# Dealing out the P @ V blocks: at most three (or four) behind each third slot instead of all that is due

## The chip, the cores and the metric

The kernel runs on one core of a Trainium2 chip. The metric is the device time of one execution in microseconds (us), median of several runs; lower is better. The engines are named as in the profile: PE (TensorE, matmuls; PEld its weight loads), DVE (VectorE), ACT (ScalarE), POOL (GpSimd), SP (SyncE, which issues nearly all DMAs).

## The reference

The input is one sequence `x` of 2048 tokens of 512 values. Two attention branches of 32 heads of 16 dimensions each are mixed by a gate per token:

```python
g = sigmoid((x * gate_w).sum(-1, keepdims=True))
a = A(x)      # full softmax attention: softmax(q k^T / 4) v over all 2048 keys, then @ A_wo
b = B(x)      # per segment of 512 tokens: causal softmax attention inside the segment,
              # blended with a memory (phi(q) M / phi(q) z) of the segments before, then @ B_wo
return g * a + (1 - g) * b
```

So for 512 queries a head of A has 2048 keys to score, a head of B 512, of which the causal mask leaves about half. All numbers are float32.

## The kernel before

**Stages.** First the projections: `x` times the weights, as high and low float32r halves, in 64 matmul slots (`slot`, L311). They end about 342 us into the profiled execution. Then comes the attention phase, which is what the change touches.

**Units and slots.** A unit is a branch, a group of four heads and a chunk `c` of 512 queries: 32 units of A and 32 of B, mostly in turn. An A unit has 64 slots (4 heads times 16 blocks of 128 keys), a B unit 10, so a pair has 74 and the phase has 2368 slots. The loop at the end of `gated_mix` runs over the slots `n`. In each it does two things:

- `score_part(n)` (L619 the matmul, L642 and L639 the exponential): scores of one key block against 512 queries into a PSUM tile `st` (three buffers), and ACT's `exp` of it into one quarter of a tile `p` (four buffers, each for four slots).
- `max_part(n + 96)` (L204 the matmul; L219, L234, L240, L244 the reduction): for a unit further on, scores into a PSUM tile `sm` (four buffers), whose row maxima DVE takes. The maximum is put into the operands of the scores later, so that `exp` needs no second pass. The last 96 slots have no such part.

The two matmuls of a slot sit on different halves of PE's rows (partitions 0 to 49 and 64 to 113) and can run side by side.

**P @ V.** When four slots of a unit have been scored, four blocks of work are put into `queue`: block `i` stands for 128 queries of all four heads against one key block, and it is due three slots later (five for B). `some_values` (L654) takes what is due and makes runs: neighbouring blocks of the same four become one run of four matmuls, one per head, each on its own 32 columns of PE (`tile_position`), with 17 weight columns (16 dimensions and a column of ones for the sum) and 128 to 512 query columns. They are float32, so each matmul is two in the trace: a run is eight matmuls, whatever its width. All runs add into one PSUM tile `ops`; after the last block of a unit ACT copies it (L679, `oraw`) and it is stored.

**What sets the order.** Every engine works its instructions in the order in which this loop emits them. `some_values` is called behind each third slot (`BURST = 3`). There it competes with `fill`: a list of output products with their due slots (L758 `fin`, eight matmuls of 512 columns each, 36 times; and L890 in the last chunk). When a fill is due, it takes that place (`filled`), P @ V is left out there, and the blocks wait. Fills come 33 slots apart in chunks 0 and 1 and 24 apart in chunk 2. `run_late` (L194, `mt_ps`) transposes finished maxima through an `st` buffer, 64 times.

Of the kernel before, what the change touches and what calls it, by code (L numbers as in the profile page):

```python
# [34 lines left out]
NU = 32  # L35
LEAD = 96
BURST = 3
RUN = 8
GAP = {"A": 3, "B": 5}
MASK_T = 8  # L40
# [6 lines left out]
def gated_mix(ctx, tc, x, xT, wqkv, a_wo, b_wq, b_wk, b_wv, b_wo, beta, gate_w, out):  # L47
# [59 lines left out]
    nS = len(slots)  # L107
# [143 lines left out]
    def run_todo(m):  # L251

        for e in [e for e in todo if e[0] <= m]:
            todo.remove(e)
            e[1]()

    def run_late(pool, tag, m):
        for e in [e for e in late if e[0] < m]:
            late.remove(e)
            transpose_max(e[1], e[2], pool, tag)  # L260
# [3 lines left out]
    def loads(m):  # L264

        m = min(m, len(maxs) - 1)
        while loaded[0] <= m:
            u, (r, i) = maxs[loaded[0]]
            if loaded[0] == first_max[u]:
                load_q(u)  # L270
            kc = u[2] if u[0] == "B" else i // 8
            if (u, kc) not in kt_:
                load_k(u, kc)
            loaded[0] += 1
# [329 lines left out]
    queue = []  # L604

    def score_part(n):

        u, j = slots[n]
        side, g, c = u
        q = qt[u]  # L610

        if j % 4 == 0:
            pt_[u, j // 4] = pp.tile([128, 4, CH], F32, tag="p", name="p")
        p = pt_[u, j // 4]
        h = (0, 2, 1, 3)[j % 4]

        def score(ps, h, b, k, n0, q0):

            nc.tensor.matmul(ps[:, n0:n0 + CH - q0], rows(k[:, :, b * 128:(b + 1) * 128], h, 50),  # L619
                             rows(q[:, :, q0:], h, 50), start=True, stop=True)  # L620

        def diagonal(x):
            nc.gpsimd.affine_select(out=x, in_=x, pattern=[[0, 4], [1, 128]], base=0, channel_multiplier=-1,  # L623
                                    compare_op=ALU.is_ge, fill=0.0)

        ps = st_ps.tile([128, CH], F32, tag="st", name="st")
        if side == "A":
            score(ps, h, j // 4 % 4, kt_[u, j // 16], 0, 0)
        else:
            k = kt_[u, c]  # L630
            if j < 8:
                score(ps, h, j // 4, k, 0, 128 * (j // 4))
                if j >= 4:
                    score(ps, h, 3, k, 384, 384)
            else:
                for f in range(2):
                    score(ps, 2 * (j - 8) + f, 2, k, 256 * f, 256)
        if side == "B" and j >= 8:
            nc.scalar.activation(p[:, 2 * (j - 8):2 * (j - 8) + 2, 0:256], ps.rearrange("p (h t) -> p h t", h=2), AF.Exp,  # L639
                                 scale=SCALE)  # L640
        else:
            nc.scalar.activation(p[:, h], ps, AF.Exp, scale=SCALE)  # L642
        if j % 4 == 3 or j == SLOTS[side] - 1:
            if side == "B":
                diagonal(p[:, :, 0:128])
                if j == 7:
                    diagonal(p[:, :, 384:])
            queue.extend((n + GAP[side], u, i) for i in range(j // 4 * 4, j + 1))
# [2 lines left out]
    PIECES = ([(0, 128 * i, 128 * i) for i in range(4)] + [(1, 128 * i, 128 + 128 * i) for i in range(3)] + [(3, 384, 384)]  # L651
              + [(2, 0, 256), (2, 128, 384)])

    def some_values(n, most=8):  # L654

        while queue and most and queue[0][0] <= n:
            _, u, i = queue.pop(0)
            most -= 1
            side, g, c = u
            w = 1  # L660
            while (queue and most and queue[0][0] <= n and queue[0][1] == u and (i + w) // 4 == i // 4
                   and (side == "A" or PIECES[i + w][0] == PIECES[i][0])):
                queue.pop(0)
                most -= 1
                w += 1
            p = pt_[u, i // 4]
            if side == "A":
                c0 = q0 = 128 * (i % 4)
                v = vt[u][:, i // 16, i // 4 % 4]
            else:  # L670
                b, c0, q0 = PIECES[i]
                v = vt[u][:, b]
            done = i + w == SLOTS[side]
            for h in range(4):
                nc.tensor.matmul(ops[32 * h:32 * h + 17, q0:q0 + 128 * w], v[:, 17 * h:17 * h + 17], p[:, h, c0:c0 + 128 * w],  # L675
                                 start=(i == 0), stop=done, tile_position=(0, 32 * h))
            if done:
                raw = ob.tile([128, CH], F32, tag="o", name="oraw")
                nc.scalar.copy(raw, ops)  # L679
                nc.sync.dma_start(od[side, c][4 * g:4 * g + 4].rearrange("h r t -> (h r) t"), raw)  # L680
                return
# [68 lines left out]
    def out_products(c, b, i):  # L750

        ps = st_ps.tile([128, D], F32, tag="st", name="fin")
        for n in range(RUN * i, RUN * i + RUN):
            side = "AB"[n // 12]
            half, o = n % 12 // 4, n % 4
            l = held["lo" if half == 0 else "hi", side, c, b]
            r = wos[side][1 if half == 1 else 0]
            nc.tensor.matmul(ps, l[:, o], r[:, o], start=(n == RUN * i), stop=(n == RUN * i + RUN - 1))  # L758
        t = fr.tile([128, D], F32, tag="res" if i == 0 else "more", name="res", bufs=2 if i == 0 else 1)
# [27 lines left out]
    for c in range(1, NCH):  # L787
        t0 = 108 * c - 84
        factors_at("M", c, t0, dend[c].rearrange("h (q t) -> (h q) t", q=4))
        for o in range(NO):  # L790
            n = t0 + 32 + 14 * o
# [120 lines left out]
    n = 0  # L912
    while n < nS or queue or waiting or beside or fill:
        for f in beside.pop(n, []):
            f()
        waiting += fill.pop(n, [])
        if n < nS:
            score_part(n)
        m = n + LEAD
        if m < nS:  # L920
            loads(m + PRE)
            max_part(m, sm_ps)
        run_todo(m)
        if n % BURST == BURST - 1 or n >= nS:

            filled[0] = bool(waiting) and not filled[0] and m < nS
            if not filled[0]:
                some_values(n)

                run_late(st_ps, "st", m + 1)  # L930
            if waiting and (filled[0] or m >= nS):
                waiting.pop(0)()
        n += 1
# [15 lines left out]
def build():  # L949
    import concourse.bacc as bacc  # L950
    nc = bacc.Bacc("TRN2", target_bir_lowering=False, num_devices=1)
    shapes = {"x": (S, D), "xT": (D, S), "wqkv": (D, 3 * D), "a_wo": (D, D), "b_wq": (D, D), "b_wk": (D, D),
              "b_wv": (D, D), "b_wo": (D, D), "beta": (H,), "gate_w": (D,)}
    args = [nc.dram_tensor(n, s, F32, kind="ExternalInput").ap() for n, s in shapes.items()]
    out = nc.dram_tensor("out", (S, D), F32, kind="ExternalOutput").ap()
    with tile.TileContext(nc) as tc:
        gated_mix(tc, *args, out)
    return nc
# [23 lines left out]
```

## Time and profile before

| | us |
|---|---|
| median of three runs | 2026.42 (2024.52 to 2027.84) |
| the profiled execution | 2020.79 |
| its span in the profile | 2019.1 |
| projections, until the first scores of the attention phase | 342 |
| attention phase, 2368 slots | 342 to 1992 |
| after the last slot | 27 |

| engine | busy us | share of the span | instructions |
|---|---|---|---|
| PE | 1929.0 | 96% | 12481 |
| PEld | 928.8 | 46% | 12481 |
| DVE | 1614.2 | 80% | 2740 |
| ACT | 1485.6 | 74% | 2905 |
| POOL | 364.0 | 18% | 566 |

A busy share of PE is read with care: matmuls are pipelined and their ends are modelled, so that a matmul waiting behind another looks busy. What an operation costs is read from starts: from the start of one to the start of what follows it. Instructions on DVE and ACT overlap too by a little (a reduction lasts 0.68 us, the next starts 0.60 us after it).

### The profile page before, as it was taken

The page shows a single profiled execution, that of the slowest core. Times are in us where ns is not written, and L with a number is a line of the kernel's source. Part 1 is how long each engine was busy: PE and PEld are TensorE (multiplying, and loading weights), DVE is VectorE, ACT ScalarE, POOL GpSimd, SP SyncE. Part 2 cuts the span into 40 slices and gives each one's busy share as a digit, 9 for nine tenths or more (in the row PEclk, how much of TensorE's full clock was granted, in tenths as well). Part 3 has the DMA queues.
Part 4 walks back from the last instruction along what each step waited for, and adds up shares of the span by engine and source line. Part 5 has one row for each costly group of instructions (what it writes and reads, how often), then busy time and mean ns, then how long its engine had stood idle before and what let it go on. Part 6 is the DMA issues. An engine that isn't in the chain of part 4 may idle for free.

```text
span 2019.1 us, 34830 instructions
## 1 busy us (share of the span) xinstructions
PE 1929.0 (96%) x12481; PEld 928.8 (46%) x12481; DVE 1614.2 (80%) x2740; ACT 1485.6 (74%) x2905; POOL 364.0 (18%) x566
## 2 busy tenths in 40 slices
PE   8999999999999999999999999999999999999996
PEld 6887765433433344444444444444444434444442
DVE  3235786998999999988888999888898998888800
ACT  3244333787888888878887888888887887877763
POOL 3000001233111112211121123111211232211240
PEclk9999998998999999999999999999998999999997
DMA  6668545355443337222221364223223552222311
GB/s 209 219 201 272 194 145 174 101 153 157 129 112 92 88 89 170 85 73 80 86 82 50 107 151 131 70 75 84 82 74 82 148 134 72 86 83 80 110 52 37
DMA packets 117483, 233.27 MB, mean 116 GB/s; under 512 B 24272, under 2 KB 38640, under 8 KB 116800
## 3 DMA queue, kind: packets, MB, share of 16 engines
q1 hardware_dynamic: 115792, 229.53, 39.1%
q8 instruction: 100, 1.64, 0.3%
q0 software_dynamic: 1232, 0.99, 0.2%
q14 instruction: 71, 0.58, 0.1%
q10 hardware_dynamic: 288, 0.52, 0.1%
HBM read 159.07 MB, written 70.66 MB: 114 GB/s over the span
## 4 chain that ended last, share of the span: by engine, by line
PE 81%; ACT 11%; DVE 4%; DMA 2%; issue 2%; POOL 0%; SPq 0%; ACTq 0%; DVEq 0%; POOLq 0%
PE ops L675 27%; PE st L619 26%; PE pr L311 12%; PE sm L204 9%; ACT p L642 8%; PE fin L758 4%; DVE pm L219 2%; PE fin L890 1%; ACT dg L230 1%; PE num L467 1%; ACT oraw L679 1%; PE mt_ps L194 1%; PE mps L498 0%; DMA qdA<-q 0%; DMA qdB<-q 0%
## 5 line engine op out<-in xcount | busy, mean ns | idle before, releaser
L219 DVE TENSOR_REDUCE pm<-sm 128x1 f32<-128x512 f32 x2048 | 1289.8, 682 | 156.8 <-PE sm L204 132.4
L642 ACT ACTIVATE p<-st 128x512 f32<-128x512 f32 x2304 | 1214.9, 609 | 211.7 <-PE sm L204 162.2
L619 PE MATMUL st<-qA,kA 50*128 50x512 f32 x2048 | 762.2, 454 | 36.2 <-ACT p L642 31.3
L204 PE MATMUL sm<-kA,qA 48*128 48x512 f32 x2048 | 785.0, 456 | 1.8 <-DVE pmB L240 0.8
L619 PEld LDWEIGHTS st<-qA,kA 50*128 50x128 f32 x2048 | 345.4, 188 | 597.7 <-ACT p L642 509.4
L675 PE MATMUL ops<-p,vA 128*17 128x512 f32 x4096 | 544.6, 607 | 0.0
L204 PEld LDWEIGHTS sm<-kA,qA 48*128 48x128 f32 x2048 | 343.9, 187 | 25.2 <-DVE pm L219 12.5
L204 PE MATMUL sm<-kB,qB 48*128 48x128 f32 (+2 forms) x896 | 176.2, 301 | 0.0
L204 PEld LDWEIGHTS sm<-kB,qB 48*128 48x128 f32 x896 | 138.4, 193 | 7.9 <-DVE pm L219 1.2
L619 PE MATMUL st<-qB,kB 50*128 50x384 f32 (+3 forms) x512 | 127.8, 348 | 12.6 <-ACT p L642 10.9
L675 PEld LDWEIGHTS ops<-p,vA 128*17 128x17 f32 x4096 | 69.9, 95 | 148.3 <-issue 137.2
L231 POOL TENSOR_SCALAR_AFFINE_SELECT dg<-dg 128x512 f32<-128x512 f32 x128 | 81.2, 635 | 277.8 <-ACT dg L230 277.6
L619 PEld LDWEIGHTS st<-qB,kB 50*128 50x128 f32 x512 | 73.9, 186 | 96.7 <-ACT p L642 81.0
L187 POOL CAST ms<-nm 128x16 fp32r<-128x16 f32 x64 | 12.6, 197 | 568.5 <-DVE nm L180 480.5
L359 DVE TENSOR_TENSOR q<-pr,q 128x512 fp32r<-128x512 f32 x64 | 44.0, 687 | 85.1 <-ACT q L352 76.7
L352 ACT CAST q<-pr 128x512 fp32r<-128x512 f32 x64 | 37.4, 585 | 94.9 <-PE pr L311 66.9
L623 POOL TENSOR_SCALAR_AFFINE_SELECT p<-p 128x512 f32<-128x512 f32 x128 | 78.5, 635 | 79.6 <-ACT p L642 77.2
L240 DVE TENSOR_REDUCE pmB<-sm 128x4 f32<-128x512 f32 x128 | 87.0, 680 | 5.3 <-PE sm L204 5.1
L675 PE MATMUL ops<-p,vB 128*17 128x512 f32 (+3 forms) x1024 | 89.5, 453 | 0.1
L234 DVE TENSOR_REDUCE pmB<-dg 128x4 f32<-128x512 f32 x128 | 86.7, 677 | 2.9 <-POOL dg L231 2.9
L230 ACT COPY dg<-sm 128x512 f32<-128x512 f32 x128 | 77.4, 605 | 5.7 <-DVE pmB L234 3.7
L765 POOL TENSOR_TENSOR res<-res 128x512 f32<-128x512 f32 x24 | 30.8, 1282 | 247.3 <-ACT res L760 247.3
(166 smaller groups left out, 1571.1 us busy)
## 6 DMA issues: line engine op xcount, KB each, us to landing
kA<-kdA SPq DMA_DIRECT2D x256, 128.0 KB
vA<-vdA SPq DMA_DIRECT2D x32, 544.0 KB
kA<-kdA SPq DMA_DIRECT2D x256, 64.0 KB
qdA<-q SPq DMA_DIRECT2D x32, 256.0 KB
kdA<-q SPq DMA_DIRECT2D x32, 256.0 KB
qdB<-q SPq DMA_DIRECT2D x32, 256.0 KB
qA<-qdA SPq DMA_DIRECT2D x64, 128.0 KB
kdB<-q SPq DMA_DIRECT2D x32, 256.0 KB
```

The costliest lines, as they stand in the source:

```text
L204: nc.tensor.matmul(ps[:, n0:n0 + n], rows(qt[u][:, :, s * 128:(s + 1) * 128], h, 48), rows(k[:, :, k0:k0 + n], h, 48), start=True, stop=True)
L219: nc.vector.tensor_reduce(pm[:, h, s, kc:kc + 1], ps, axis=AX.X, op=ALU.max)
L230: nc.scalar.copy(dg, blocked(ps))
L231: nc.gpsimd.affine_select(out=dg, in_=dg, pattern=[[0, 4], [-1, 128]], base=0, channel_multiplier=1, compare_op=ALU.is_ge, fill=MASKED)
L234: todo.append((m + MASK_T, lambda: nc.vector.tensor_reduce(to, dg.rearrange("p (h s) t -> p h s t", h=2), axis=AX.X, op=ALU.max)))
L240: nc.vector.tensor_reduce(pm[:, 1, h, 3:7], blocked(ps), axis=AX.X, op=ALU.max)
L311: nc.tensor.matmul(ps, l(a, k), r(b, k), start=(n == 0), stop=(n == 11))
L619: nc.tensor.matmul(ps[:, n0:n0 + CH - q0], rows(k[:, :, b * 128:(b + 1) * 128], h, 50), rows(q[:, :, q0:], h, 50), start=True, stop=True)
L623: nc.gpsimd.affine_select(out=x, in_=x, pattern=[[0, 4], [1, 128]], base=0, channel_multiplier=-1, compare_op=ALU.is_ge, fill=0.0)
L642: nc.scalar.activation(p[:, h], ps, AF.Exp, scale=SCALE)
L675: nc.tensor.matmul(ops[32 * h:32 * h + 17, q0:q0 + 128 * w], v[:, 17 * h:17 * h + 17], p[:, h, c0:c0 + 128 * w], start=(i == 0), stop=done ...
L758: nc.tensor.matmul(ps, l[:, o], r[:, o], start=(n == RUN * i), stop=(n == RUN * i + RUN - 1))
```

## The change

`some_values` gets its limit from the caller: three blocks behind each third slot, four where the queue holds more than eight, and eight again once all slots are done. A run that is cut by the limit goes on at the next call; what is due, the order of the blocks and the place of the fills stay as they are.

```diff
+MOST = 3
...
-    def some_values(n, most=8):
+    def some_values(n, most):
...
             filled[0] = bool(waiting) and not filled[0] and m < nS
             if not filled[0]:
-                some_values(n)
+                some_values(n, MOST + (len(queue) > 8) if n < nS else 8)
```

The new line 38 moves all later lines of the kernel down by one: L675 before is L676 after.

## The prediction, made before the changed kernel had run

> **What bounds the kernel now.** I read the page first: PE 96% busy, DVE 80%, and the groups of the attention phase.
>
> ```profile
> PE 1929.0 (96%) x12481; PEld 928.8 (46%) x12481; DVE 1614.2 (80%) x2740; ACT 1485.6 (74%) x2905; POOL 364.0 (18%) x566
> ...
> L219 DVE TENSOR_REDUCE pm<-sm 128x1 f32<-128x512 f32 x2048 | 1289.8, 682 | 156.8 <-PE sm L204 132.4
> L642 ACT ACTIVATE p<-st 128x512 f32<-128x512 f32 x2304 | 1214.9, 609 | 211.7 <-PE sm L204 162.2
> ```
>
> PE looks like the bound, but the reductions (one per slot) lose 157 us waiting for PE. Whether that is lack of PE time or bad order is told by a quiet stretch. The timeline of PE and that of DVE, columns start, length, engine, line, tiles, count; lines of the second matmul of each slot are left out:
>
> ```profile
> 612.30 0.50 PE L619 MATMUL st<-qA,kA 50*128 50x512 f32 x1
> ...
> 613.19 1.05 PE L675 MATMUL ops<-p,vA 128*17 128x512 f32 x8
> 614.17 0.50 PE L619 MATMUL st<-qA,kA 50*128 50x512 f32 x1
> ...
> 615.08 1.05 PE L675 MATMUL ops<-p,vA 128*17 128x512 f32 x8
> 616.06 0.50 PE L619 MATMUL st<-qA,kA 50*128 50x512 f32 x1
> ...
> 617.25 0.50 PE L619 MATMUL st<-qA,kA 50*128 50x512 f32 x1 [0.21 <-ACT p L642]
> ...
> 617.74 0.50 PE L619 MATMUL st<-qA,kA 50*128 50x512 f32 x1
> ...
> 618.23 0.50 PE L619 MATMUL st<-qA,kA 50*128 50x512 f32 x1
> ```
>
> ```profile
> 609.91 3.67 DVE L219 TENSOR_REDUCE pm<-sm 128x1 f32<-128x512 f32 x6
> ```
>
> Call three slots a group and the P @ V behind it a burst. Twelve A slots bring three bursts of four blocks and a fourth group with none. A group with a burst takes 614.17 to 616.06 = 1.89 us: 0.91 until the burst starts, 0.98 in it. In the group behind the empty place PE is held up: its score matmuls stand 0.49 apart (617.25, 617.74, 618.23), at ACT's and DVE's pace. The cycle from 609.90 to 617.25 takes 7.35. DVE needs (3.67 - 0.68) / 5 = 0.598 per reduction, 7.18 for twelve. PE needs 4 x 0.91 + 3 x 0.98 = 6.58. So a quiet stretch is bound by DVE but loses 0.17 of 7.35: three full bursts in a row (1.89 against DVE's 3 x 0.598 = 1.79) use up DVE's lead, and the empty place cannot give it back, the buffers being full.
>
> Around an output product it is worse:
>
> ```profile
> 841.88 1.16 PE L758 MATMUL fin<-wohA,lA 128*128 128x512 f32 x4 [0.31 <-ACT p L642]
> 842.88 1.07 PE L758 MATMUL fin<-wolA,hA 128*128 128x512 f32 x4
> 843.88 0.49 PE L619 MATMUL st<-qA,kA 50*128 50x512 f32 x1
> ...
> 845.05 1.91 PE L675 MATMUL ops<-p,vA 128*17 128x512 f32 x16
> 846.90 0.50 PE L619 MATMUL st<-qA,kA 50*128 50x512 f32 x1
> ```
>
> ```profile
> 844.47 0.69 DVE L240 TENSOR_REDUCE pmB<-sm 128x4 f32<-128x512 f32 x1 [1.40 <-PE sm L204]
> ...
> 847.47 2.48 DVE L219 TENSOR_REDUCE pm<-sm 128x1 f32<-128x512 f32 x4 [1.11 <-PE sm L204]
> ```
>
> The group with the product takes 3.27 us (840.61 to 843.88), the next, with eight blocks at once, 3.02. DVE stands still 1.40 and then 1.11 us. The 33 slots from this product to the next (840.61 to 862.85) take 22.24, DVE needing 33 x 0.598 = 19.7.
>
> **The change, part by part.** Built, the changed program differs on PE alone: ACT, DVE, POOL and SP issue the same instructions, as many of each. On PE, bursts go from 579 to 753 (+174), runs from 640 to 1137 (+497); blocks and columns stay. Twelve quiet A slots now bring bursts of 3, 1+3, 1+2 and 2 blocks. Behind a product no burst has more than four.
>
> Price of a cut run. A has none, but B does (its diagonal cuts runs):
>
> ```profile
> 785.37 1.06 PE L675 MATMUL ops<-p,vB 128*17 128x384 f32 x16
> 786.36 0.50 PE L619 MATMUL st<-qA,kA 50*128 50x512 f32 x1
> ...
> 787.27 0.62 PE L675 MATMUL ops<-p,vB 128*17 128x256 f32 x8
> 787.83 0.50 PE L619 MATMUL st<-qA,kA 50*128 50x512 f32 x1
> ```
>
> A burst of 384 + 128 columns takes 0.99, one of 512 0.98: the second run costs about 5 ns (0.988 against 0.983 unrounded). A burst of 256 takes 0.56, one of two full runs 1.85 (845.05 to 846.90), so a block costs (1.85 - 0.98) / 4 = 0.217 and entering and leaving a burst about 0.12. Three blocks are then 0.77, an estimate between 0.56 and 0.98. The trace has no burst that begins with the narrow run; between the 384 + 128 row (nothing) and the whole 0.56 less two blocks (0.12 more) I take nothing, since 384 + 128 + 256 in one burst takes 1.42, the 256 behind the 128 at full pace.
>
> *Quiet stretches* (slots 0 to 755, 1122 to 1346, 1714 to 1939: 1207 slots, 801 us). PE now needs 4 x 0.91 + 0.77 + 0.99 + 0.78 + 0.56 = 6.74 per twelve, 0.16 more, still under 7.18, and its lead is refilled in every cycle (groups of 1.68, 1.90, 1.69, 1.47 against 1.79). The 0.17 goes: 1207 / 12 x 0.17 = 17. A pair of units (74 slots) takes 47.0 at best, though its 74 reductions and two small ones need 44.5 (74 x 0.598 + 0.27): of the 2.5, 1.05 is this pattern, the rest lies around the transposes (mt_ps) and B. Those instructions stay; a lead may cover some. Ends 0 and 16 pairs x 1.45 = 23; I take 8, nearer nothing, since the transpose's own wait for an `st` buffer stays.
>
> *Products.* 33 slots after: 11 x 0.91 + 2.36 for the product (3.27 - 0.91) + 33 x 0.217 + 10 x 0.12 = 20.7, and 0.2 for groups with B's keys (0.94 rather than 0.91): 20.9, now over DVE's 19.7. PE is never far enough ahead to be held up, so this is nearly what it takes: gain at most 1.3, I take 1.2, for 24 products: 29. Those 24 slots apart take 17.0 (1664.56 to 1681.54); after: 8 x 0.91 + 2.36 + 24 x 0.217 + 7 x 0.12 + 0.2 = 15.9; I take 0.9 x 12 = 11. Ends for both: 0 and 45.
>
> *What gets later.* Blocks wait longer, so tiles `p` are held longer. The nearest reuse was 3 slots behind the last burst that reads the tile; now it is 0 in two tiles, 1 in six. From one slot on the burst stands ahead of the score on PE and nothing waits; at 0 ACT waits one burst: 2 x 1 = 2 lost; bound 24 x 1 for all of two slots and less. DVE never queues behind it; POOL's masks and SP's queue are not passed. The copy `oraw` moves by a burst or two (4 us), ahead of loads 18 slots (11 us) later: nothing. In the last 96 slots, without reductions, 8 bursts more cost 8 x 0.12 = 1.
>
> **Sum:** 17 + 8 + 29 + 11 - 2 - 1 = 62. The profiled execution took 2020.8 (span 2019.1), 5.6 under the median 2026.4; taken from that, 1959, on the scale of the median 2026.4 - 62 = **1964**.
>
> **Rivals.**
>
> *Every burst is paid* (the other side). If PE had no slack, each of the 174 bursts would cost its 0.12 and the slower first pair behind it (0.34 from the first to the second maximum product, 614.18 to 614.52, then 0.23), 0.22 in all, and each run 5 ns: 38 + 2.5 = 41 more, 2067. For it: PE's 96% and its 81% of the chain that ended last. Against: the 0.49 spacings above. It decides when a cut run costs over (7.35 - 6.74) / 3 = 0.2 us; B's rows show 0.005.
>
> [...]
>
> *Only quiet stretches gain*: the products' 2.36 is waited out as before, since four buffers hold no more than 2.4 us of DVE's work. 17 + 8 - 3 = 22: 2004. For it: no lead survives 3.27 us. Against: the second stall (1.11) comes from the eight blocks alone.
>
> *All slack comes back*: 17 + 23 + 45 = 85: 1941.
>
> **How the numbers follow.** Forecast 0.66 (1945 to 1990), all slack 0.10, quiet stretches only 0.10, bursts paid 0.10, issue 0.01, nothing measurable 0.03. The range 1930 to 2010 holds the first three but for their ends. Faster by over 0.2% (what a measurement of this kernel can tell) 0.85, within 0.2% 0.04, slower 0.11.
>
> **What would show it.** Right: bursts of 384 at 0.77 and 128 + 384 at 0.99; the stall of 1.11 behind a product gone, that of 1.40 not larger; the stage 1107 to 1255 (147.5 us, 225 slots) at about 142, 1255 to 1513 (258.6) at about 243; reductions' idle time down from 157 to about 100. Wrong: a gap inside a burst between narrow and wide runs; score matmuls waiting for ACT behind bursts where now they do not; reductions waiting in every group.

## The result, and the profile after

The changed kernel takes 1968.11 us (median of four runs, 1963.67 to 1975.58) against 2025.47 (2019.15 to 2027.84) of the kernel before: ratio 0.9725, 95% interval 0.9687 to 0.9764. A second set of runs (e8 below) gave 0.9723 (0.9691 to 0.9756). The forecast was 1964, with a range of 1930 to 2010.

The page of the profile after (the profiled execution took 1963.67, its span is 1961.9), the same three lines as before:

```profile
PE 1903.3 (97%) x16457; PEld 1029.7 (52%) x16457; DVE 1606.2 (82%) x2740; ACT 1487.2 (76%) x2905; POOL 365.1 (19%) x566
...
L220 DVE TENSOR_REDUCE pm<-sm 128x1 f32<-128x512 f32 x2048 | 1284.6, 682 | 112.6 <-PE sm L205 96.6
L643 ACT ACTIVATE p<-st 128x512 f32<-128x512 f32 x2304 | 1220.4, 607 | 172.5 <-PE sm L205 114.3
```

PE has 3976 matmuls more (497 runs of eight) and a busy time that is shorter by 26 us: more matmuls did not make it busier. The idle time of DVE before its reductions falls from 157 to 113 us.

A quiet stretch, DVE's timeline of the kernel after:

```profile
745.74 3.07 DVE L220 TENSOR_REDUCE pm<-sm 128x1 f32<-128x512 f32 x5
748.73 0.68 DVE L245 TENSOR_REDUCE pmB<-sm 128x4 f32<-128x512 f32 x1
749.32 2.47 DVE L220 TENSOR_REDUCE pm<-sm 128x1 f32<-128x512 f32 x4
751.83 0.22 DVE L181 TENSOR_REDUCE nm<-pm 128x16 f32<-128x64 f32 x1
751.97 3.07 DVE L220 TENSOR_REDUCE pm<-sm 128x1 f32<-128x512 f32 x5
```

Five reductions in 3.07 are (3.07 - 0.68) / 4 = 0.598 apart, and no line carries an idle time: DVE goes from one group to the next without a break. This is the bound that the prediction named for such a stretch.

Behind an output product, timelines of PE and DVE in the kernel after (the first score and the burst of the next two groups, then the reductions of the same stretch):

```profile
852.27 0.50 PE L620 MATMUL st<-qA,kA 50*128 50x512 f32 x1
...
853.45 1.05 PE L676 MATMUL ops<-p,vA 128*17 128x512 f32 x8
854.43 0.50 PE L620 MATMUL st<-qA,kA 50*128 50x512 f32 x1
...
855.33 0.84 PE L676 MATMUL ops<-p,vA 128*17 128x384 f32 x8
856.10 0.50 PE L620 MATMUL st<-qA,kA 50*128 50x512 f32 x1
```

```profile
852.84 1.89 DVE L220 TENSOR_REDUCE pm<-sm 128x1 f32<-128x512 f32 x3 [1.34 <-PE sm L205]
855.00 1.29 DVE L220 TENSOR_REDUCE pm<-sm 128x1 f32<-128x512 f32 x2 [0.28 <-PE sm L205]
```

The first stall is what it was (1.34; before 1.40), the second is 0.28 where eight blocks made it 1.11. Over all 36 products the medians are 1.26 (before 1.33) and 0.28 (before 0.95). A burst of three takes 856.10 - 855.33 = 0.77, as estimated.

Where the 57 us between the two profiles lie, by stages cut at the same slots:

| slots | before us | after us | less | forecast less | PE time lost at half clock, before and after |
|---|---|---|---|---|---|
| until slot 0 | 342.1 | 343.4 | -1.3 | 0 | 0.0, 2.0 |
| quiet: 0-755, 1122-1346, 1714-1939 | 501.7, 147.5, 152.0 | 487.2, 144.1, 145.6 | 24.3 | 25 | 20.5, 6.5 |
| with products: 756-1121, 1347-1713, 1940-2271 | 263.5, 258.6, 249.3 | 250.0, 250.7, 239.5 | 31.2 | 40 (and 2 lost) | 10.2, 1.7 |
| last 96 slots and the end | 104.4 | 101.4 | 3.0 | -1 | 10.6, 7.4 |

The last column comes from the clock that the traces show as granted to PE: it is 1, but for stretches at 0.5, and half the length of such a stretch is PE time lost. In all it is 41.3 us before and 17.6 after, so some 24 of the 57 us is the most that the clock can have taken directly.

### The profile page after: what moved, and what is told of

The parts are those of the page before. It is cut to its first block, busy times and chain, and to the rows that moved or that the text cites. A ratio compares the mean times of both kernels' runs of the same rounds, so it can differ in the third digit from the quotient of the medians.

```text
span 1961.9 us, 42783 instructions
## 1 busy us (share of the span) xinstructions
PE 1903.3 (97%) x16457; PEld 1029.7 (52%) x16457; DVE 1606.2 (82%) x2740; ACT 1487.2 (76%) x2905; POOL 365.1 (19%) x566
## 4 chain that ended last, share of the span: by engine, by line
PE 86%; ACT 6%; DVE 3%; DMA 3%; issue 2%; POOL 0%; SPq 0%; ACTq 0%; DVEq 0%; POOLq 0%
PE ops L676 28%; PE st L620 26%; PE sm L205 13%; PE pr L312 11%; ACT p L643 4%; PE fin L759 4%; PE fin L891 1%; DVE pm L220 1%; ACT dg L231 1%; PE num L468 1%; DMA kdB<-q 1%; PE mt_ps L195 1%; PE mps L499 0%; DMA qdB<-q 0%; DMA qdA<-q 0%
## 5 line engine op out<-in xcount | busy, mean ns | idle before, releaser
L220 DVE TENSOR_REDUCE pm<-sm 128x1 f32<-128x512 f32 x2048 | 1284.6, 682 | 112.6 <-PE sm L205 96.6
L205 PE MATMUL sm<-kA,qA 48*128 48x512 f32 x2048 | 774.0, 454 | 1.9 <-DVE pmB L241 0.8
L620 PE MATMUL st<-qA,kA 50*128 50x512 f32 x2048 | 726.5, 444 | 10.4 <-ACT p L643 8.7
L620 PEld LDWEIGHTS st<-qA,kA 50*128 50x128 f32 x2048 | 338.2, 186 | 446.7 <-ACT p L643 357.2
L676 PE MATMUL ops<-p,vA 128*17 128x128 f32 (+3 forms) x8008 | 570.8, 389 | 0.0
L205 PEld LDWEIGHTS sm<-kA,qA 48*128 48x128 f32 x2048 | 339.4, 185 | 36.5 <-DVE pm L220 20.5
L676 PEld LDWEIGHTS ops<-p,vA 128*17 128x17 f32 x8008 | 163.2, 96 | 167.9 <-issue 153.3
L620 PE MATMUL st<-qB,kB 50*128 50x384 f32 (+3 forms) x512 | 120.5, 343 | 4.4 <-ACT p L643 3.4
L676 PE MATMUL ops<-p,vB 128*17 128x128 f32 (+3 forms) x1088 | 89.0, 421 | 4.1 <-issue 1.9
```

What stands on the lines that cost most here:

```text
L205: nc.tensor.matmul(ps[:, n0:n0 + n], rows(qt[u][:, :, s * 128:(s + 1) * 128], h, 48), rows(k[:, :, k0:k0 + n], h, 48), start=True, stop=True)
L220: nc.vector.tensor_reduce(pm[:, h, s, kc:kc + 1], ps, axis=AX.X, op=ALU.max)
```

## Experiments

Two theories stood at the start. **Order**: DVE starves less because full bursts no longer follow one another and none has eight blocks. **Clock**: the trace of before shows 13 places in which P @ V matmuls last over 0.8 us rather than 0.6, PE's granted clock being 0.5 there instead of 1, that of after three; the difference could be theirs, and chance. Below, such a place is called slow. The kernels below differ from the changed one by the lines shown; quiet pairs are 74 slots of undisturbed quiet (slots 76 to 149 and 298 to 371).

**e1, the kernel before once more.**

```diff
-                some_values(n, MOST + (len(queue) > 8) if n < nS else 8)
+                some_values(n, 8)
```

> The kernel before once more (limit eight), for its profile and the noise. Two theories on the 57 us. Order: DVE starves less, since full bursts no longer follow one another and no burst has eight blocks; of the 57, about 15 in quiet stretches, 25 to 30 behind the products, 10 to 15 from fewer stretches at a lower PE clock (the trace of before has 13 places where P @ V matmuls last over 0.8 us, that of after 3). Then this run is at 2025 (2017 to 2033), ratio 1.00, and its profile has again about ten slow places. Clock: the slow places come and go by chance, and most of the difference is theirs; then this profile may well have three or four of them, and a span near 1990.

Measured: 2022.9, ratio 0.9996 (0.9973 to 1.0019). Twelve slow places, at other times than in the first profile; quiet pairs 47.0 and 47.0. The number of slow places belongs to this order of the work and is no chance.

**e2, limit four, no run of A cut.**

```diff
-                some_values(n, MOST + (len(queue) > 8) if n < nS else 8)
+                some_values(n, 4 if n < nS else 8)
```

> Limit four throughout: the bursts of eight behind a product are gone, but no run of A is cut, and three bursts of four with an empty place stay the pattern of a quiet stretch. Order: the second stall of DVE behind a product (1.1 us, 18 bursts of eight) goes, 0.5 to 0.7 for each of 36 products, about 20 in all: 2005 (1997 to 2013), and the quiet stage of 225 slots stays at 146 to 148. Rival, the cut into three does it all: within 5 of before, 2020 to 2027. Rival, the cap does it all: 1970.

Measured: 2007.55, ratio 0.9914 (0.9888 to 0.9940), 17 us. The quiet stage of 225 slots stays at 147.3; the stages with products go to 257.1, 256.3 and 245.7, 12 less in sum (the profiled execution, 2015.48, is the slowest of its ten). The cap alone is worth about a third of the whole, and only behind products.

**e3, the same bursts, every run of A cut into one block and three.**

```diff
-                   and (side == "A" or PIECES[i + w][0] == PIECES[i][0])):
+                   and (side == "A" and (i + w) % 4 != 1 or side == "B" and PIECES[i + w][0] == PIECES[i][0])):
...
+                some_values(n, 8)
```

> Bursts as before (limit eight), but every run of A is cut into one block and three: 512 runs more, no burst moved. It measures the price of a cut run alone. By B's rows (5 ns for each): 2.6 us, lost in the noise, 2022 to 2033. Rival, a narrow run in front costs 0.1 or more (its weight loads stand bare): 51 us or more, 2076.

Measured: 2021.91, ratio 0.9992 (0.9969 to 1.0015): between 6 us less and 3 more for 512 cut runs, 6 ns for each at most. In the trace of after, some 200 bursts of 128 + 384 columns take 0.988 (median), one of 512 takes 0.983. Narrow runs cost next to nothing here.

**e4, eight blocks again right behind a product.**

```diff
+            after_fill = filled[0]
             filled[0] = bool(waiting) and not filled[0] and m < nS
             if not filled[0]:
-                some_values(n, MOST + (len(queue) > 8) if n < nS else 8)
+                some_values(n, 8 if n >= nS or after_fill else MOST + (len(queue) > 8))
```

> Three blocks (four above eight) as in the change, but the burst right behind a product may take eight again: the change without its cap where it is most needed. Order: quiet stretches keep their 15 and the fewer slow places, the products lose a part of theirs: 1980 (1970 to 1995). Rival, the gain is all behind the products: 2015 or more.

Measured: 1977.42, ratio 0.9773 (0.9738 to 0.9807). The quiet stages are those of the change (487.4, 144.5, 146.0), the others 253.9, 252.7 and 248.6, 15 more in sum. Of these, 9 stand in the last stage, where half clock took 10.2 us of PE time and 1.7 in the change. So the gain is not all behind products, and by the medians the cap there is worth about ten.

**e5, behind each fourth slot.**

```diff
-BURST = 3
+BURST = 4
...
-                some_values(n, MOST + (len(queue) > 8) if n < nS else 8)
+                some_values(n, 4 + 2 * (len(queue) > 8) if n < nS else 8)
```

> P @ V behind each fourth slot instead of each third, limit four (six where more than eight wait): 543 bursts rather than 753, most of four whole blocks, and hardly an empty place (16). Order: in a quiet stretch PE needs three times 1.13 + 0.98 for twelve slots, 6.3, DVE 7.18; quiet pairs as in the change, 46.1; behind products PE has 19.7 to do for 33 slots where the change has 20.9, so some 0.4 for each of 36 products more: 1952 (1940 to 1965), fewer than five slow places. Rival, a longer group is worse, because DVE's four buffers run dry in a burst and ACT's three fill up in four scores: 1980 or more.

Measured: 2102.34, ratio 1.0381 (1.0351 to 1.0410). The expectation failed, and the rival that stood beside it holds. PE's timeline of this kernel, one group of four slots and the burst behind it:

```profile
657.30 0.49 PE L620 MATMUL st<-qA,kA 50*128 50x512 f32 x1
...
657.63 0.63 PE L620 MATMUL st<-qA,kA 50*128 50x512 f32 x2
...
658.54 0.50 PE L620 MATMUL st<-qA,kA 50*128 50x512 f32 x1 [0.27 <-ACT p L643]
...
658.97 0.63 PE L676 MATMUL ops<-p,vB 128*17 128x256 f32 x8
```

Three scores start within 0.57, the fourth 0.67 after the third: there are three buffers `st`, and the fourth score waits 0.27 for ACT's `exp` to free one. The burst starts behind that score, at 658.97; in the profiles of before and after, too, none starts inside a group (where only A is scored, 3, 6 or 9 scores stand between one burst or product and the next). On the page of this kernel ACT's exponentials wait 279 us in all, in that of the change 173, and DVE's reductions 203 rather than 113. That three slots stand between bursts fits the three buffers; I had counted 0.24 for each further score.

**e6, behind each second slot.**

```diff
-BURST = 3
+BURST = 2
...
-                some_values(n, MOST + (len(queue) > 8) if n < nS else 8)
+                some_values(n, 2 + (len(queue) > 8) if n < nS else 8)
```

> P @ V behind each second slot, limit two (three where more than eight wait): the evenest deal, 1119 bursts. Order: entering and leaving a burst is paid where PE is the bound. Twelve quiet slots need six times (0.34 + 0.24 + 0.09 + 0.12 + 0.43) = 7.3, just over DVE's 7.18: quiet pairs 46.5 to 47.5; 33 slots with a product need 22.2 where the change needs 20.9: 40 more in all than the change, 2008 (1990 to 2020). Rival, evenness is all that counts: 1968 or less.

Measured: 2010.46, ratio 0.9930 (0.9906 to 0.9954); quiet pairs 48.0 and 47.8, a little over the range given. 366 bursts more than the change cost 42 us, 0.12 for each: what entering and leaving a burst was priced at. In slots 756 to 1713, where both kernels have the full clock throughout, it is 20.3 us for 148 bursts more, 0.14 for each. The evenest deal is not the best; it is PE that is short here: the reductions' idle time is 145 us, 113 in the change.

**e7, a run that adds nothing in the empty places.** Weights of zero, 128 columns of a gate tile as the moving side; the result is unchanged. (`zero` is a tile of zeros; `taken` notes whether the call of `some_values` took a block, and whether its unit goes on.)

```diff
...
+    def idle_run():
+        for h in range(4):
+            nc.tensor.matmul(ops[32 * h:32 * h + 17, 0:128], zero, gate["A", 0], start=False, stop=False,
+                             tile_position=(0, 32 * h))
...
+                some_values(n, 8)
+                if not taken[0] and taken[1] and m < nS:
+                    idle_run()
```

> Bursts as before (limit eight), but in 138 of the empty places PE adds a run of 128 columns with weights of zero to the accumulator: it adds nothing to the result, and no block of P @ V is moved. It asks whether the slow places of PE's clock come from three or more microseconds of score matmuls with no P @ V or product between them: in the six profiles so far 32 of the 34 places that began before 1860 us stand behind such a gap, and no more than 2 behind one under 3.0. If so, the slow places in the attention phase fall from about ten to under four and 10 to 20 us go, though the order stays as bad: 2010 (2002 to 2017), undisturbed quiet pairs still 47.0. Rival, the gaps only stand beside the cause: ten slow places, 2022 to 2030.

Measured: 2013.4, ratio 0.9953 (0.9938 to 0.9969): 9.5 us less (6 to 13) for 138 runs of work without use. The gaps of 3.0 us and over, from a burst or product to the next, fell from about 45 to 19 (before 1860 us), the slow places between 365 and 1860 us from 9 and 7 (in the profiles of before and e1) to 4. Quiet pairs stay at 47.1 and 47.1. Four places are one more than expected; the direction and the size of the time hold.

**e8, the changed kernel once more.**

> The changed kernel once more, for a narrower interval and a second profile: 1968 (1960 to 1976), ratio 0.9725, three or four slow places of PE's clock, quiet pairs 46.1. If the fewer slow places were chance, this profile has about ten and a span near 1980.

Measured: 1967.78, ratio 0.9723 (0.9691 to 0.9756). Four slow places, three of them in the first 20 us of the attention phase (two of three in the first profile); quiet pairs 46.1 and 46.1.

**e9, three nearly always.**

```diff
-                some_values(n, MOST + (len(queue) > 8) if n < nS else 8)
+                some_values(n, MOST + (len(queue) > 10) if n < nS else 8)
```

> Three blocks, four only where more than ten wait: bursts as many as in the change (753), evener, but the blocks wait longer: the burst that last reads a tile p stands at the slot that reuses the tile, or behind it, for 21 tiles rather than 2. It weighs evenness against lateness. Order: quiet stretches are at DVE's pace already, so evenness brings nothing there, and each of the 21 tiles holds ACT up by at most 1 us: 1972 (1964 to 1990). Rival, evenness still pays behind products: 1960 or less.

Measured: 1962.1, ratio 0.9685 (0.9651 to 0.9719), the lowest of all; its interval overlaps that of the change (e8), but beside e8, measured with it, it stands 5.7 lower, and all six of its runs lie below all six of e8. Neither number fits well. The stages say more: with products 248.9, 249.7 and 238.9 where the change has 250.0, 250.7 and 239.5, quiet ones of 143.0 and 144.2 where it has 144.1 and 145.6. The clock is full in these stages but for the last with products. So evenness pays about one us in each, in quiet stretches too, which the order theory had at nothing; and holding 21 tiles longer shows nowhere.

## Why the prediction was right, point by point

- **The bound.** Quiet stretches bound by DVE with a loss from the order: shown. Quiet pairs go from 47.0 to 46.1, and between the transposes DVE runs almost without a break. The other side's mechanism, every burst being paid, is refuted for the change and shown where it must hold, in e6.
- **The price of a cut run** (5 ns from B's rows): shown by e3 and by the trace of after. That PE's issue binds (0.01 in the chances) falls with it: PE has 16457 matmuls and as many weight loads where it had 12481 of each, in a span of 1961.9 us instead of 2019.1. What issuing one of them takes no run shows.
- **The pattern's 17 us in quiet stretches and the 8 around transposes**: together about 15, both mis-sized. Nine pairs without a slow place in the first quiet stage (from before, e1 or e3, which have the same order of bursts, against after) are shorter by 0.4 to 1.2, 0.9 in the mean; for 16.3 pairs that is 15. Where they gain is read from DVE: how much more than 0.598 lies between the starts of its reductions, summed over a pair, the mean of eight of the nine (in slots 594 to 667 DVE has next to nothing to lose). In the first 46 slots of a pair, which are plain pattern, 0.50 falls to 0.12; the prediction's 0.17 per twelve slots is 0.65 there. In the other 28, with the transposes and the slots of B, 2.3 falls to 1.8; the pattern (0.40) and the transposes (0.5) were to give 0.9. What share each of the two has in these 28 slots isn't shown. At the transposes of slots 76 to 149 the stalls shrink (the first two lines are from before, the next two from after, the same places); elsewhere, as behind slot 500 in the kernel after (the last two), they stay:

```profile
433.99 0.69 DVE L219 TENSOR_REDUCE pm<-sm 128x1 f32<-128x512 f32 x1 [0.44 <-PE st L619]
...
438.04 1.38 DVE L219 TENSOR_REDUCE pm<-sm 128x1 f32<-128x512 f32 x2 [0.38 <-PE sm L204]
```

```profile
432.30 0.69 DVE L220 TENSOR_REDUCE pm<-sm 128x1 f32<-128x512 f32 x1 [0.23 <-PE st L620]
...
436.14 1.37 DVE L220 TENSOR_REDUCE pm<-sm 128x1 f32<-128x512 f32 x2 [0.17 <-PE sm L205]
```

```profile
669.61 1.29 DVE L220 TENSOR_REDUCE pm<-sm 128x1 f32<-128x512 f32 x2 [0.54 <-PE sm L205]
671.45 0.69 DVE L220 TENSOR_REDUCE pm<-sm 128x1 f32<-128x512 f32 x1 [0.55 <-PE sm L205]
```

- **What made up the rest**: the quiet stages fell by 24, not by 15, and the rest is PE's clock, which the prediction had not priced at all. The same 74 slots (150 to 223) take 52.5 in the profile of before, with two slow places, and 48.1 in that of e1, with none; slots 224 to 297 take 48.8 without and 49.9 with one. Half clock took 5.1 us of PE time in the first case and 1.7 in the second, so 0.65 to 0.86 of it shows in the time. The 24 us in the table's last column then make 15 to 20 of the 57: an estimate, not measured by itself. e7 shows the effect (9.5 us) with about half of the places gone.
- **The products' 40 us**: mis-sized, 31, of which up to 8.5 are the clock's. The step that failed is "PE is never far enough ahead to be held up, so this is nearly what it takes". For the 33 slots from one product to the next 20.9 was worked out; after the change the shortest takes 21.6 and the median is 22.7 (before 22.0 and 23.4). The first stall stays, the second shrinks to 0.28 rather than to nothing, and in slots 756 to 1121 the weight loads of scores still wait 61 us for ACT to free a buffer (89 before); how much of that wait costs time isn't shown. The stage 1255 to 1513 was to fall from 258.6 to 243 and fell to 250.7. Of the part behind products, e2 puts 12 on the cap of four; the rest comes with the even bursts and the clock.
- **What gets later** (2 lost) and the last slots (1 lost): e9, with ten times as many late tiles, lost nothing that can be seen, so the 2 were too dear. The last 96 slots and the end gained 3.0, but half clock took 3.2 us less of PE time there, which leaves the 1 open.
- **What would show it**: bursts of 384 take 0.77 and those of 128 + 384 take 0.99, as named. Of the stages forecast at 142 and 243, the first went 3.4 of 5.5 us of the way (144.1), the second half-way; the reductions' idle time was to be about 100 and is 112.6.
- **The total**: 1964 against 1968 is in part luck. The order of the work brought some 37 to 42 of the 62 us forecast for it, and the clock, which stood in no term, made up most of what was missing.

## What to carry to other kernels

Where one engine works for two others through a few buffers, in the order of one loop, look at the size of its longest piece of other work against those buffers, not at its sum: 57 us came from dealing out the same columns in pieces of 0.34 to 0.99 us rather than 0, 0.98 and 1.85, a part of them by way of PE's clock. The spacing was bounded on both sides here: each extra entry into the other kind of matmul cost 0.12 us (e6), and the fourth score of a group waited 0.27 for one of three buffers (657.30 to 658.97, e5). Before counting on a filled gap, count the buffers of every consumer that must work during it.

## What the runs showed that I had not expected

PE's clock falls to 0.5 behind stretches in which PE is busy with matmuls. In e1, PE's timeline from the end of one burst to the next, and the scores behind it:

```profile
520.84 0.50 PE L620 MATMUL st<-qA,kA 50*128 50x512 f32 x1
...
522.54 0.46 PE L620 MATMUL st<-qA,kA 50*128 50x512 f32 x1
...
523.85 1.63 PE L676 MATMUL ops<-p,vA 128*17 128x512 f32 x8
525.41 0.79 PE L620 MATMUL st<-qA,kA 50*128 50x512 f32 x1
```

From 520.84 to 523.85 there are only score matmuls, on 48 and 50 rows where an output product has 128, the last three scores 0.51 and 0.62 apart; the burst behind them lasts 1.56 instead of 0.98. In the six profiles of before, after and e1 to e4, until 1860 us and leaving out the start of the attention phase, 32 of the 34 slow places stand behind a gap of 3.0 us or more without P @ V or a product; of the 173 gaps of that length 32 have one, of over 3600 shorter ones two. The change leaves one such gap in its profile where before has 44. A gap is not the only way to a slow place: e6 has none of that length, and one slow place (1811 us).

Which of the long gaps are followed by a slow place can be read from the traces as well. Within a profile, the stretches at clock 0.5 all start a whole multiple of 3.41 us apart (in that of before 10, 40, 45 and 156 steps behind the first and so on, to 490), and until 1860 us each lasts 3.41 us or a multiple, as if the clock were set anew at fixed steps. Of the gaps in these six profiles that fill at least 3.0 us of one such step, 33 of 39 have a stretch at 0.5 starting at the end of the step; of over 3700 other gaps, seven.

PE wasn't idle in such a gap: from 520.84 to 523.85 it is busy for 2.90 of 3.01 us. What in such a step lowers the clock no run here shows.
